# Attention and an MLP mixer on one core: ten of 18 channel-MLP token groups deferred, and run as seven block products

## The chip, the cores and the metric

The kernel runs on one core of a Trainium2 chip. The core has a tensor engine (PE in the profile; its weight loads are listed apart as PEld), VectorE (DVE), ScalarE (ACT), GpSimd (POOL) and SyncE (SP), which here only issues DMAs; ScalarE issues DMAs too. Each engine works through its own queue in order and waits on semaphores. Matmuls write PSUM, which VectorE and ScalarE read. The metric is the time of one execution in microseconds on the device, the median of several runs.

## The reference

All arrays are float32 (the weights reach the device as they are stored on the host). Eight batches, eight heads, 576 tokens, head size 64.

```python
scores = scale * q @ k.T                      # (8, 8, 576, 576)
thresh = max(scores, -1) - tau
scores = where(scores >= thresh, scores, -1e9)
attn   = softmax(scores)                      # sum + 1e-9
x = (attn @ v) with heads side by side        # (8, 576, 512)

h  = relu(x.T @ w_tok1) @ w_tok2              # token MLP, 576 -> 256 -> 576
u  = x + h.T
h2 = relu(u @ w_ch1) @ w_ch2                  # channel MLP, 512 -> 1536 -> 512
out = u + h2
```

## The kernel before

The order of the work is written out by hand and kept as written. Attention is cut into 144 **units** of 128 query rows and two heads: 8 batches x 2 halves x 9. One turn of the main loop (`for u in range(...)`) does, for unit u:

- `scores(u)` (L306): score matmuls into two PSUM tiles; VectorE takes the row maximum (L311), GpSimd makes the bias (L312).
- `norm(u-1)` (L335 to L339): reciprocals on VectorE, products on GpSimd.
- `fill(0.4)`: channel and token MLP steps (below).
- `turn_blocks(u-2)`: VectorE transposes the weights of unit u-2 within 32x32 blocks into a third of the tile T (L369). After every third unit SyncE issues 16 DMAs, each a block row and column of T, into eT (L378); there is one eT buffer.
- `weigh(u)`: two ScalarE passes (L321, L328), with three times `fill(0.2)` between and behind them.
- loads of q and k for later pairs on ScalarE's queue (L105), of v on SyncE's (L114).
- `values(...)`: for a set of three units, two turns after its `turn_blocks`, the value products on the tensor engine (L413, L418), which read eT; ScalarE copies them to xT, the activations x transposed (L423).

In batch 0 the transposes go over the tensor engine (L357), not over DMAs.

After a batch's last value product `push(b)` makes its later work a list of steps, each with a cost in us written in the code: the token MLP (`token_mlp`: five transposes L449, two first-layer steps L456, eight second-layer steps L466 with an add on VectorE, L470; 18.8 in all), mixed with what is left of the list, and then groups of 256 tokens of the **channel MLP** (`channel_mlp`). Two batches lie side by side in xT: 1152 tokens, four groups and a half. An even batch adds the first two groups, an odd batch the other two and a half. A group has twelve steps `ch1` (four matmuls of 256 columns, L509, and a Relu on ScalarE, L510; cost 1.7 each) and eight steps `ch2` (three matmuls of 512 columns, L530, cost 2.6 each; after four of them an add on VectorE, L542, and the store, L549): 41.4. At its second `ch1` the group's activations are turned on VectorE (L493) and moved by 16 DMAs on SyncE (L499).

`fill(share)` adds `share * quota` to a credit and issues steps until the credit is used up. The quota is set by `push`, so that `KEEP` is left when the next batch's steps come:

```python
    KEEP = 45.0
    KEEP_FIRST = 20.0
        ...
        quota = (sum(c for c, _ in todo) - (KEEP if b else KEEP_FIRST)) / (UB - 1)
```

UB is 18, a batch's units. `push(0)` runs in turn 20, `push(b)` for later b at the end of turn 18b + 21 (39 for batch 1). After the loop `fill(1.0)` issues all that is left: the last batch's token MLP, the leftover and the groups (6, 2), (6, 3) and the half group (6, 4), which `ch2_last` (L557, L564, L569) ends.

Of the kernel before, what the change touches and what calls it, by code (L numbers as in the profile page):

```python
# [21 lines left out]
def kernel(  # L22
# [43 lines left out]
    SCALE = 1.0 / 8.0  # L66

    const = ctx.enter_context(tc.tile_pool(name="const", bufs=1))
    ld = ctx.enter_context(tc.tile_pool(name="ld", bufs=2))
    work = ctx.enter_context(tc.tile_pool(name="work", bufs=2))  # L70
    small = ctx.enter_context(tc.tile_pool(name="small", bufs=6))
    ps_sc = ctx.enter_context(tc.tile_pool(name="ps_sc", bufs=2, space=bass.MemoryType.PSUM))
    ps_tr = ctx.enter_context(tc.tile_pool(name="ps_tr", bufs=2, space=bass.MemoryType.PSUM))


# [19 lines left out]
    def load_qk(n, eng, parts=range(8), blocks=(range(S // 32),) * 2):  # L95


        b, p = pairs[n]
        if n not in loaded:
            loaded[n] = [ld.tile([P, S // 32, 32], F32, tag=tag, bufs=1, name=f"{tag}_{n}") for tag in ("lq", "lk")]  # L100
        for part in parts:
            i, which = divmod(part, 2)
            h, c = divmod(i, 2)
            lo, hi = blocks[which].start, blocks[which].stop
            eng[which].dma_start(  # L105
                out=loaded[n][which][32 * i : 32 * i + 32, lo:hi],
                in_=(q, k)[which][b, 2 * p + h, 32 * lo : 32 * hi, 32 * c : 32 * c + 32].rearrange("(n t) d -> t n d", t=32),
            )

    def load_v(n):  # L110

        b, p = pairs[n]
        lv = ld.tile([P, NK, D], F32, tag="lv", bufs=4, name=f"lv_{n}")
        nc.sync.dma_start(out=lv, in_=v[b].rearrange("h s d -> (h s) d")[2 * S * p : 2 * S * p + 2 * S, :].rearrange("(c p) d -> p c d", p=P))  # L114
        vals[n] = lv

# [166 lines left out]

    def prep(n, parts=((0, 0, S // 32), (1, 0, S // 32))):
        if n not in heads:
            heads[n] = [work.tile([P, S], F32, tag=name, name=f"{name}_{n}") for name in ("qT", "kT")]
        for which, lo, hi in parts:
            nc.vector.transpose(
                out=heads[n][which][:, 32 * lo : 32 * hi], in_=loaded[n][which][:, lo:hi].rearrange("p n d -> p (n d)")
            )  # L290
# [24 lines left out]
    def weigh(u):  # L315
        sc, bias = st.pop(u)
        rs = small.tile([P, 2], F32, tag="rs", name=f"rs_{u}")
        e = work.tile([P, 2 * S], F32, tag="e", bufs=3, name=f"e_{u}")
        for h in range(2):
            eh = e[:, S * h : S * h + S].rearrange("p (f x) -> p f x", f=2)  # L320
            nc.scalar.activation(out=eh, in_=sc[h][:, :, 0:HS], func=AF.Prelu, bias=bias[:, h : h + 1], scale=SCALE, alpha=STEEP)  # L321
        st[u] = e, rs

        if b_now:
            fill(0.2)
        for h in range(2):
            eh = e[:, S * h : S * h + S]
            nc.scalar.activation(out=eh, in_=eh, func=AF.Exp, bias=ntau, accum_out=rs[:, h : h + 1])  # L328
            if b_now:
                fill(0.2)  # L330
# [13 lines left out]
    def turn(u, third):  # L344

        b, p0, t = units[u]
        key, place = (b, p0, t // GU), t % GU
        e = st[u]

        if third == 0 and place == 0:  # L350
            eTs[key] = work.tile([P, NK, GU * P], F32, tag="T", name=f"eT_{u}")
        if third == 2:
            st.pop(u)
        ps = ps_tr.tile([P, MAIN], F32, tag="tr", name=f"tr{third}_{u}")[:, 0 : 3 * P].rearrange("p (c x) -> p c x", c=3)
        for c in range(3):
            k0 = (3 * third + c) * P
            nc.tensor.transpose(out=ps[:, c, :], in_=e[:, k0 : k0 + P], identity=ident)  # L357
        on = nc.scalar.copy if third == 1 else nc.vector.tensor_copy
        on(out=eTs[key][:, 3 * third : 3 * third + 3, P * place : P * place + P], in_=ps)

    def turn_blocks(u):
# [2 lines left out]
        key, place = (b, p0, t // GU), t % GU  # L364
        e = st.pop(u)
        if place == 0:
            Ts[key] = work.tile([P, 4, GU, NK * 32], F32, tag="T", name=f"T_{u}")
        T = Ts[key]
        nc.vector.transpose(  # L369
            out=T[:, :, place, :].rearrange("p a (c x) -> p c a x", c=NK), in_=e.rearrange("p (c a x) -> p c a x", c=NK, a=4)  # L370
        )
        if place == GU - 1:
            del Ts[key]
            eT = work.tile([P, GU, 4, NK * 32], F32, tag="eT", bufs=1, name=f"eT_{u}")
            eTs[key] = eT.rearrange("p n i (c x) -> p (n i) c x", c=NK)
            for a in range(4):
                for i in range(4):
                    nc.sync.dma_start(out=eT[32 * a : 32 * a + 32, :, i, :], in_=T[32 * i : 32 * i + 32, a, :, :])  # L378
# [105 lines left out]
    def channel_mlp(b, uT, i):  # L484
# [63 lines left out]
                    nc.vector.tensor_copy(out=o, in_=flat)  # L548
                nc.sync.dma_start(out=out[b : b + 2].rearrange("b s d -> (b s) d")[t0 : t0 + P, :], in_=o)  # L549

        def ch2_last(half):

            t0 = GR * i
            w = DM // 2
            ps = ps_mm.tile([P, w], F32, tag="mm", name=f"c2_{b}_{i}_h{half}")
            for j in range(NJ):
                nc.tensor.matmul(  # L557
                    ps, lhsT=s["g"][:, j, 0:P], rhs=wc2[:, j, w * half : w * half + w], start=(j == 0), stop=(j == NJ - 1)
                )
            if half == 0:  # L560
                move_u()
            o = s["us"][:, half].rearrange("q a x -> q (a x)")[:, 0:w]
            cs = slice(NCC // 2 * half, NCC // 2 * half + NCC // 2)
            nc.vector.tensor_add(  # L564
                out=o.rearrange("q (c k d) -> q c k d", c=NCC // 2, k=4),
                in0=ps.rearrange("q (c k d) -> q c k d", c=NCC // 2, k=4),
                in1=s["ut"][:, 0].rearrange("q k (c d) -> q c k d", c=NCC)[:, cs],
            )
            nc.sync.dma_start(out=out[b : b + 2].rearrange("b s d -> (b s) d")[t0 : t0 + P, w * half : w * half + w], in_=o)  # L569

        if b == B - 2 and n == P:
            return [(0.0067 * n, lambda j=j: ch1(j)) for j in range(NJ)] + [(5.2, lambda half=half: ch2_last(half)) for half in range(2)]
        return [(0.0067 * n, lambda j=j: ch1(j)) for j in range(NJ)] + [
            (2.6 if part or b else 3.0, lambda t=t, part=part: ch2(t, part)) for t in range(nt) for part in range(4)
        ]
# [1 line left out]
    def move_u():  # L577
        while moves:
            moves.popleft()()

    KEEP = 45.0
    KEEP_FIRST = 20.0
# [17 lines left out]
    def push(b):  # L603
# [10 lines left out]
            todo.extend(old[:n] + [step])  # L614
            del old[:n]
        todo.extend(old)
        for i in range(2) if b % 2 == 0 else range(2, (2 * S + GR - 1) // GR):
            todo.extend(channel_mlp(b - b % 2, uT, i))
        quota = (sum(c for c, _ in todo) - (KEEP if b else KEEP_FIRST)) / (UB - 1)


# [26 lines left out]
    for u in range(len(units) + LAG + 4):  # L648
# [88 lines left out]

        if back and wt % GU == 0 or not on:
            move_u()
    need(len(pieces) - 1)  # L740
    quota = 1e9
    fill(1.0)
# [1 line left out]
_INS = ['q', 'k', 'v', 'tau', 'moe_w_tok1', 'moe_w_tok2', 'moe_w_ch1', 'moe_w_ch2']  # L744
_OUTS = [((8, 576, 512), 'float32')]
# [25 lines left out]
```

## Time and profile before

| | us |
|---|---|
| runs: median (lowest to highest of 3) | 1352.09 (1351.51 to 1353.36) |
| profiled execution, first to last instruction | 1349.9 |
| tensor engine busy, first layer of the channel MLP (L509) | 400.1 |
| tensor engine busy, second layer (L530, and L557) | 379.0, 10.5 |
| tensor engine busy, scores (L306) | 190.3 |
| tensor engine busy, value products (L413, L418) | 46.9, 136.8 |
| tensor engine busy, token MLP (L456, L466) | 72.4, 75.2 |
| VectorE row maximum (L311), block transposes (L369) | 204.4, 171.9 |
| ScalarE passes (L321, L328) | 199.8, 221.1 |
| DMA eT<-T: 672 issues, median to landing | 2.3 each |

A line of the profile names the code line, the engine, the operation, and output<-inputs by the program's tile names. Durations of matmuls overlap, since they are pipelined: what one costs is the distance from start to start. A float32 matmul of the code shows as two records. Unit 40 starts at 272.1 us, unit 142 at 1140.3, the last value product ends at 1182.7, and the work up to 1242.7 is the list's leftover and the token MLP of batch 7; then come the last two and a half groups.

### The profile page before, as it was taken

The numbers are of one execution on the slowest core, as the hardware profiler recorded it, in microseconds if no ns is written. First come the engines' busy times: TensorE is split into PE (matmuls) and PEld (weight loads), VectorE is DVE, ScalarE is ACT, GpSimd is POOL, SyncE is SP. The second block draws the span as 40 slices with busy tenths as digits, with TensorE's granted clock in tenths as the row PEclk, the third lists the DMA queues.
The fourth block names the chain that finished last, engine by engine and source line by source line (L and its number), as shares of the span: only waits on it lengthen the run. The fifth ranks groups of instructions, "written<-read, shape, count | busy, mean of one in ns | idle before, by whom it ended". The sixth has DMA issues, their size and how long they took to land.

```text
span 1349.9 us, 17890 instructions
## 1 busy us (share of the span) xinstructions
PE 1306.6 (97%) x6186; PEld 817.1 (61%) x6186; DVE 592.2 (44%) x1026; ACT 585.1 (43%) x1299; POOL 352.5 (26%) x683
## 2 busy tenths in 40 slices
PE   7888899999999999999999999999999999999999
PEld 5565556547474666655665567565656566575677
DVE  6878874445443435434334445434443454201000
ACT  6777654444445435443434444354333454120110
POOL 4565652222222213222222222222221222100000
PEclk8998999999999999999999999999999999999999
DMA  5535764535353544543345435535443453400000
GB/s 123 120 87 127 199 168 97 127 94 136 83 133 89 114 109 96 126 109 88 86 107 125 98 85 123 125 82 115 109 102 83 114 118 79 112 22 17 23 24 32
DMA packets 296746, 135.31 MB, mean 100 GB/s; under 512 B 204816, under 2 KB 289552, under 8 KB 296656
## 3 DMA queue, kind: packets, MB, share of 16 engines
q1 hardware_dynamic: 168944, 118.27, 34.4%
q10 hardware_dynamic: 127712, 15.90, 7.4%
q8 instruction: 49, 0.80, 0.3%
q14 instruction: 41, 0.34, 0.1%
HBM read 43.25 MB, written 9.44 MB: 39 GB/s over the span
## 4 chain that ended last, share of the span: by engine, by line
PE 86%; DVE 6%; DMA 3%; ACT 2%; SPq 1%; issue 1%; POOL 1%; ACTq 0%; DVEq 0%; POOLq 0%
PE c L530 26%; PE c L509 26%; PE sc L306 11%; PE pv L418 9%; PE t L456 5%; PE t L466 4%; PE pv L413 3%; DVE mx L311 2%; PE tx L449 1%; DMA lk<-in_k_dram 1%; ACT e L321 1%; SPq L378 1%; PE c_h L557 1%; DVE T L369 1%; DVE high L211 1%
## 5 line engine op out<-in xcount | busy, mean ns | idle before, releaser
L509 PE MATMUL c<-xT,wc 128*128 128x256 f32 (+1 forms) x1920 | 400.1, 362 | 0.1
L311 DVE TENSOR_REDUCE mx<-sc 128x1 f32<-128x576 f32 x288 | 204.4, 750 | 444.3 <-PE sc L306 443.2
L530 PE MATMUL c<-wc,g 128*128 128x512 f32 x840 | 379.0, 597 | 0.0
L509 PEld LDWEIGHTS c<-xT,wc 128*128 128x128 f32 x1920 | 334.9, 191 | 69.3 <-issue 29.7
L312 POOL TENSOR_SCALAR bias<-mx,toff 128x1 f32<-128x1 f32 x288 | 81.1, 282 | 775.6 <-DVE mx L311 722.7
L321 ACT ACTIVATE e<-sc,bias 128x576 f32<-128x576 f32 x288 | 199.8, 739 | 182.5 <-POOL bias L312 176.7
L530 PEld LDWEIGHTS c<-wc,g 128*128 128x128 f32 x840 | 154.7, 190 | 176.1 <-issue 172.4
L328 ACT ACTIVATE e<-e,ntau 128x576 f32<-128x576 f32 x288 | 221.1, 771 | 0.0
L339 POOL TENSOR_SCALAR e<-e,rr 128x576 f32<-128x576 f32 x288 | 214.3, 756 | 14.8 <-ACT g L510 2.6
L510 ACT ACTIVATE g<-c 128x256 f32<-128x256 f32 (+1 forms) x240 | 86.7, 361 | 296.5 <-PE c L509 283.4
L306 PE MATMUL sc<-kT,qT 64*128 64x288 f32 (+1 forms) x1280 | 190.3, 433 | 6.9 <-ACT e L321 5.9
L369 DVE STREAM_TRANSPOSE T<-e 128x1152 f32<-128x1152 f32 x126 | 171.9, 1364 | 5.5 <-DMA eT<-T 2.9
L306 PEld LDWEIGHTS sc<-kT,qT 64*128 64x128 f32 (+1 forms) x1280 | 105.2, 178 | 92.2 <-issue 57.2
L418 PE MATMUL pv<-eT,lv 128*64 128x384 f32 (+1 forms) x1024 | 136.8, 408 | 0.0
L418 PEld LDWEIGHTS pv<-eT,lv 128*64 128x64 f32 x1024 | 76.9, 138 | 49.9 <-issue 42.1
L423 ACT COPY xT<-pv 128x384 f32<-128x384 f32 (+1 forms) x56 | 21.0, 400 | 164.6 <-PE pv L418 159.5
L466 PE MATMUL t<-w,a 128*128 128x288 f32 x256 | 75.2, 421 | 8.2 <-DVE xT L470 4.8
L542 DVE TENSOR_TENSOR us<-c,ut 128x512 f32<-128x512 f32 x26 | 17.9, 690 | 137.5 <-PE c L530 122.7
L456 PE MATMUL t<-x_sb,w 128*128 128x512 f32 (+1 forms) x180 | 72.4, 549 | 0.0
L466 PEld LDWEIGHTS t<-w,a 128*128 128x128 f32 x256 | 45.9, 192 | 30.2 <-issue 10.5
L470 DVE TENSOR_TENSOR xT<-xT,t 128x288 f32<-128x288 f32 x64 | 28.3, 446 | 70.6 <-PE t L466 69.9
L328 ACT ACTIVATION_READ_ACCUMULATOR e<-e,ntau 128x1 f32 x288 | 56.7, 197 | 0.0
(51 smaller groups left out, 571.2 us busy)
## 6 DMA issues: line engine op xcount, KB each, us to landing
eT<-T SPq DMA_DIRECT2D x672, 108.0 KB, 2.3
scratch<-in_moe_w_ch_dram SPq DMA_DIRECT2D x24, 512.0 KB, 3.7
lv<-in_v_dram SPq DMA_DIRECT2D x32, 288.0 KB, 3.5
out_dram<-us SPq DMA_DIRECT2D x35, 256.0 KB, 2.2
lk<-in_k_dram ACTq DMA_DIRECT2D x109, 72.0 KB, 2.7
lq<-in_q_dram ACTq DMA_DIRECT2D x106, 72.0 KB, 2.3
ut<-us SPq DMA_DIRECT2D x192, 32.0 KB, 1.9
lk<-in_k_dram SPq DMA_DIRECT2D x19, 72.0 KB, 3.2
```

The costliest lines, as they stand in the source:

```text
L306: nc.tensor.matmul(sc[h][rows, f, 0:HS], lhsT=qT[r, cols], rhs=kT[r, HS * f : HS * f + HS], start=True, stop=True)
L311: nc.vector.tensor_reduce(out=mx[:, c], in_=sc[h][:, :, 0:HS], axis=AX.XY, op=ALU.max)
L321: nc.scalar.activation(out=eh, in_=sc[h][:, :, 0:HS], func=AF.Prelu, bias=bias[:, h : h + 1], scale=SCALE, alpha=STEEP)
L328: nc.scalar.activation(out=eh, in_=eh, func=AF.Exp, bias=ntau, accum_out=rs[:, h : h + 1])
L339: nc.gpsimd.tensor_scalar(out=eh, in0=eh, scalar1=rr[:, h : h + 1], scalar2=1.0, op0=ALU.mult, op1=ALU.mult)
L369: nc.vector.transpose(out=T[:, :, place, :].rearrange("p a (c x) -> p c a x", c=NK), in_=e.rearrange("p (c a x) -> p c a x", c=NK, a=4))
L418: nc.tensor.matmul(to[r], lhsT=lv[:, j, :], rhs=e[j], start=False, stop=(c == NI - 1), skip_group_check=True)
L456: nc.tensor.matmul(to, lhsT=w1[:, t, P * m : P * m + P], rhs=x_sb[:, t, cols], start=(t == 0), stop=(t == NT - 1))
L466: nc.tensor.matmul(to, lhsT=a[:, m, P * c : P * c + P], rhs=w2[:, m, HS * f : HS * f + HS], start=(m == 0), stop=(m == NTK - 1))
L509: nc.tensor.matmul(ps, lhsT=wc1[:, j, c, :], rhs=uT[:, c, GR * i : GR * i + n], start=(c == 0), stop=(c == NCC - 1))
L510: nc.scalar.activation(out=s["g"][:, j, 0:n], in_=ps, func=AF.Relu)
L530: nc.tensor.matmul(flat, lhsT=s["g"][:, j, P * t : P * t + P], rhs=wc2[:, j, :], start=(j == 0 and b > 0), stop=(j == NJ - 1), skip_group_ ...
```

## The change

Only eight of the groups are still put into the list (`NOW`). The rest, ten groups' worth of tokens, waits: groups of finished batches are written to device memory (`spill`, at the end of a turn, on SyncE), those of the last batch pair stay in xT. After attention the tiles of attention are given up (`attn.close()`; its pools now lie on the right side of the memories), and the waiting tokens are taken in five blocks of 512. Both layers of a block are products of 2 x 2 blocks, and each is made of seven block products and sums instead of eight products: for `ch1(j)` seven pairs of matmuls of 256 columns, 6 x 14 in a block; for `ch2` seven parts of six matmuls of 256 columns, twice. Sums of weights and of activations are made on VectorE ahead (`sums`, the two in-place `sub` calls, `sums_u`), sums of products while they are in PSUM. Two of the accumulators (`y` and `z`) are read after their first product and then added to by a second one. The last addition of u is made on GpSimd (`late_add`). `ch2_last` goes. KEEP, the quota's formula and the main loop's order stay.

```diff
-    ld = ctx.enter_context(tc.tile_pool(name="ld", bufs=2))
+    attn = ctx.enter_context(ExitStack())
+    att = attn.enter_context(tc.tile_pool(name="att", bufs=2, side="right"))
+    ps_sc = attn.enter_context(tc.tile_pool(name="ps_sc", bufs=2, space=bass.MemoryType.PSUM, side="right"))
+    dram = ctx.enter_context(tc.tile_pool(name="dram", bufs=1, space=bass.MemoryType.DRAM))
...
+    NOW = {(0, 0), (0, 1), (0, 2), (2, 0), (2, 2), (4, 0), (4, 2), (6, 0)}
+    kept = deque()
+    spilled = {}
+
+    def spill():
+
+        while kept:
+            b, i = kept.popleft()
+            n = min(GR, 2 * S - GR * i)
+            d = dram.tile([P, NCC, n], F32, name=f"spill_{b}_{i}")
+            nc.sync.dma_start(out=d, in_=xTs[b][:, :, GR * i : GR * i + n])
+            spilled[b, i] = d
...
-        for i in range(2) if b % 2 == 0 else range(2, (2 * S + GR - 1) // GR):
-            todo.extend(channel_mlp(b - b % 2, uT, i))
+        ready = [(b - b % 2, i) for i in (range(2) if b % 2 == 0 else range(2, (2 * S + GR - 1) // GR))]
+        if b < B - 1:
+            todo.append((0.0, lambda: kept.extend(g for g in ready if g not in NOW)))
+        for g in ready:
+            if g in NOW:
+                todo.extend(channel_mlp(g[0], uT, g[1]))
         quota = (sum(c for c, _ in todo) - (KEEP if b else KEEP_FIRST)) / (UB - 1)
...
+        spill()
     need(len(pieces) - 1)
+    attn.close()
+    end = ctx.enter_context(tc.tile_pool(name="end", bufs=1, side="right", reuse_waits="tile"))
+    ps_x = ctx.enter_context(tc.tile_pool(name="ps_x", bufs=4, space=bass.MemoryType.PSUM, side="right", reuse_waits="tile"))
+    HJ, HC, HD = NJ // 2, NCC // 2, DM // 2
...
+    groups = [
+        [(0, 3), (2, 1)],
+        [(2, 3), (4, 1)],
+        [(4, 3), (6, 1)],
+        [(6, 2), (6, 3)],
+        [(0, 4), (2, 4), (4, 4), (6, 4)],
+    ]
...
+        def sums_u(self):
+            t = self.t = end.tile([P, 4, HC, GR], F32, tag="t", name=f"t_{self.n}")
+            sub(t[:, 0], self.block(0, 1), self.block(0, 0))
+            sub(t[:, 1], self.block(1, 1), t[:, 0])
+            sub(t[:, 2], self.block(1, 1), self.block(0, 1))
+            sub(t[:, 3], self.block(1, 0), t[:, 1])
...
+        def ch1(self, j):
...
+            self.product(y, list(zip(w(0, 0), u(0, 0))))
+            nc.scalar.copy(out=p1, in_=y)
+            self.product(x4, list(zip(w(1, 1), us(3))))
+            self.product(y, list(zip(w(0, 1), u(1, 0))), False)
+            nc.scalar.activation(out=c11, in_=y, func=AF.Relu)
+            self.product(x6, list(zip(ws(1), us(1))))
+            add(u2, x6, p1)
+            self.product(x7, list(zip(w(1, 0), us(2))))
+            add(u3, x7, u2)
+            self.product(z, list(zip(ws(0), us(0))))
+            add(c21, x4, u3)
+            add(c22, z, u3)
+            self.product(z, list(zip(ws(2), u(1, 1))), False)
+            nc.scalar.activation(out=self.gb[:, j, :], in_=self.gb[:, j, :], func=AF.Relu)
+            add(c12, z, u2)
+            nc.scalar.activation(out=c12, in_=c12, func=AF.Relu)
...
+        def ch2(self, m, part):
...
+            elif part == 5:
+                self.z = self.psum("tr", f"oz_{self.n}_{m}")
+                prod(self.z, s[:, 0], w2s[:, 0])
+                add(o(1, 1), four(self.z), four(u3))
+                late_add(1, 1)
+                store(1)
+            else:
+                prod(self.z, s[:, 2], side2(1, 1), start=False)
+                add(o(0, 1), four(self.z), four(u2))
+                late_add(0, 1)
+                store(0)
+
+    lates = [Late(n) for n in range(len(groups))]
+    lates[0].load()
     quota = 1e9
+    rest = list(todo)
+    todo.clear()
+    for step in rest:
+        todo.append(step)
+        if sums:
+            todo.append((0.0, sums.pop(0)))
     fill(1.0)
+    sub(side1(1, 0), side1(0, 0), side1(1, 0))
+    sub(side2(0, 1), side2(1, 1), side2(0, 1))
...
+    lates[0].sums_u()
+    for late in lates:
+        if late.n + 1 < len(lates):
+            lates[late.n + 1].load()
+        for j in range(HJ):
+            late.ch1(j)
+            if j in (1, 3):
+                late.turn_u(j // 2)
+        for m in range(2):
+            for part in range(7):
+                late.ch2(m, part)
+                if m == 0 and part == 4 and late.n + 1 < len(lates):
+                    lates[late.n + 1].sums_u()
```

`side1` and `side2` are views of a quarter of the weights wc1 and wc2; `add` and `sub` are VectorE tensor operations; `product` issues the matmuls of one block product. `turn_u` turns the activations of half a block and moves them with 16 DMAs on SyncE, as before for a group.

## The prediction

> **What bounds the kernel now.** I read the page's busy shares and slices first, then the chain, then the tensor engine's, SyncE's and VectorE's timelines where attention runs with little other work, and last the windows around long waits.
>
> ```profile
> span 1349.9 us, 17890 instructions
> PE 1306.6 (97%) x6186; PEld 817.1 (61%) x6186; DVE 592.2 (44%) x1026; ACT 585.1 (43%) x1299; POOL 352.5 (26%) x683
> PE   7888899999999999999999999999999999999999
> PEclk8998999999999999999999999999999999999999
> ...
> PE 86%; DVE 6%; DMA 3%; ACT 2%; SPq 1%; issue 1%; POOL 1%; ACTq 0%; DVEq 0%; POOLq 0%
> ```
>
> The tensor engine (PE) bounds the whole: from slice 6 on it is busy at 90% or more. So fewer products look like time saved. But that holds because channel products fill every wait of attention, and the change takes most of them out of there. What attention costs without them must be read where filling was thinnest, in batch 1:
>
> ```profile
> 228.61 1.24 PE L306 MATMUL sc<-kT,qT 64*128 64x288 f32 x8
> 229.78 3.72 PE L509 MATMUL c<-xT,wc 128*128 128x256 f32 x16
> ...
> 247.99 0.55 PE L413 MATMUL pv<-eT,vl 128*64 128x192 f32 x4 [1.76 <-DMA lq<-in_q_dram]
> ...
> 251.39 0.51 PE L306 MATMUL sc<-kT,qT 64*128 64x288 f32 x2
> ```
>
> ```profile
> 232.93 12.72 SPq L378 DMA_DIRECT2D eT<-T  x16
> ```
>
> Three units make a cycle. Scores of its first unit start at 228.61; VectorE's third transpose T of the set ends at 232.9, 4.3 us later; then SyncE issues 16 moves eT<-T one after the other; the value product needs all of them and starts at 247.99, with PE idle for 1.76 us. The lq named there is a DMA whose landing the burst shares a wait with; the last move was issued at about 245.1 and lands 2.3 us later (page row of eT<-T), which is the wait. Scores of the next cycle stand behind the value product on PE's queue. So this cycle is a loop of 22.8 us that no arithmetic sets. An undisturbed burst is hardly shorter:
>
> ```profile
> 272.14 1.20 PE L306 MATMUL sc<-kT,qT 64*64 64x288 f32 x16
> ...
> ```
>
> ```profile
> 276.44 10.32 SPq L378 DMA_DIRECT2D eT<-T  x16
> ```
>
> 10.32/16 = 0.645 us each, whatever PE does. Over the trace's 42 bursts, first issue to last landing is 11.9 to 15.5 us, mean 13.2 (moves held behind q and k loads make the difference).
>
> **The loop's length.** 4.3 + 13.2 + 0.3 (landing to product) + 3.4 (value product, 247.99 to 251.39) = **21.2 us per cycle**. PE's own work per cycle is three scores (1.17 each, 228.61 to 229.78), 3.4, and three quotas: 6.9 + 3 x quota. The quota follows from push() with the code's own costs (token MLP 18.8, a full group 41.4, 42.2 in the first batch pair):
> - Batch 1, both kernels: about 4.6, work 20.7. Just below the loop, as the trace shows.
> - Before, later: 5.0 in batch 2, then 5.5 and 7.0 in turn; work 21.9 to 27.9. PE sets the pace, the burst is covered.
> - After, batch 2: (6.2 left + 18.8 + 42.2 - 45)/17 = 1.3; work 10.8.
> - After, batches 3 to 7: (41.5 + 18.8 + 41.4 - 45)/17 = 3.3; work 17.1 (17 x 3.3 of 18 leaves the 41.5 again).
> So the loop takes over as the bound in every cycle after push(1), which runs at the end of unit 39; the cover that hid the bursts is gone.
>
> **The sum, against the profiled 1349.9.**
> 1. Up to the scores of unit 40: **272.1**, unchanged.
> 2. Units 40 to 141, 34 cycles x 21.2 = **720.8**. Before, they end near 1140.
> 3. Clock. Waits of PE rise to 4 us a cycle (21.2 - 17.1), in batch 2 to about 6 (its three units can't go faster than 3.9 each, since scores wait for Prelu to empty their PSUM). The rows of a 4.4 us wait at 107:
>
> ```profile
> 107.00:111.00 4.00, 0.00 (x0) 0.00 (x0) 3.90 (x9) 2.08 (x4) 0.89 (x4) 0.98 0.94 234
> 111.00:118.00 7.00, 6.72 (x25) 3.15 (x27) 5.87 (x9) 5.08 (x12) 4.03 (x4) 0.52 0.43 102
> ```
>
>    The seventh number after the stretch's busy times, 0.98 and 0.52, is the granted clock: a wait of 4.4 us was paid with some 6.8 us at half speed, 3.4 us of work. Waits of 1.8 (at 157.7 and 246.2) cost nothing. Bounds 0 and 3.4 per cycle; waits of 4 lie nearer the costly row, but only the part on value product and scores counts, so 0.5 for 28 cycles and 2.0 for the six of batch 2: **26**. Below nothing is excluded: waiting gives no clock.
> 4. Units 142 to the last value product: one more loop, then a burst that waits for the single eT buffer: 21.2 + 13.2 + 0.3 + 3.4 = **38.1**.
> 5. Leftover group and token MLP of batch 7: **60.0**, as from 1182.7 to 1242.7 now. The six VectorE sums of weights are put among its first steps and are hidden by it.
> 6. Handover. VectorE has behind the last leftover step its add (0.69, row of L542), two in-place differences of 1536 columns and four of 512. From 0.425 at 256 columns (L564) and 0.69 at 512: 1.75 and 0.69, sum 6.95; PE covers it with one product pair of 0.86, and halves its clock after. 6.3 + 1.7 = **8.0**.
> 7. The five blocks. Rates come from the end of the kernel before, first eight and then six records between neighbours:
>
> ```profile
> 1211.80 1.89 PE L509 MATMUL c<-xT,wc 128*128 128x256 f32 x8
> 1213.52 1.13 PE L466 MATMUL t<-w,a 128*128 128x288 f32 x4
> ...
> 1220.73 2.74 PE L530 MATMUL c<-wc,g 128*128 128x512 f32 x6
> 1223.31 1.13 PE L466 MATMUL t<-w,a 128*128 128x288 f32 x4
> ```
>
>    1.72/4 = 0.43 a product of 256 columns, 2.58/3 = 0.86 of 512 (two records each). A block: first layer 6 x 14, second 2 x 42, 168 x 0.43 = 72.2; five, 361.2. The same work before: 10 x (48 x 0.43 + 24 x 0.86) = 412.8 and 2.8 for half groups. The saving of an eighth, 54, is real in products. Against it, z is read by VectorE between its two products with no work between them on PE, 30 times in the first layer and 10 in the second. What such a turn costs:
>
> ```profile
> 301.51 0.78 DVE L470 TENSOR_TENSOR xT<-xT,t 128x288 f32<-128x288 f32 x2
> ...
> 301.98 1.24 PE L466 MATMUL t<-w,a 128*128 128x288 f32 x4 [1.26 <-DVE xT L470]
> ```
>
>    Matmul drain 0.17 (mean 0.597 less spacing 0.43), start 0.04, add 0.425, release 0.05, slower first matmul 0.11: 0.79. Four times VectorE does the next block's sums first (4 x 0.65): 1.7. So 36 x 0.79 + 4 x 1.7 = 35.2. The other waits (y after ScalarE's copy) have a product pair between and about 0.1 to spare; if they miss, 30 x 0.8 more. Sum **396.4**, only 19 below the work it replaces.
> 8. After the last matmul: 3.1 now, and a GpSimd add of 256 columns, about 0.75 (half of L225's 1.43 for 512): **3.9**.
>
> Spills (nine, at most 512 KB, one issue each), their loads and the turns of us (0.6 us an issue, 20 us per block of 79) stand on SyncE outside the bursts, at nothing; a spill just ahead of a burst would cost its transfer, about 3 us, once a batch.
>
> Sum 1525.3, and 2.2 outside the span (1352.1 less 1349.9): **1528 us**.
>
> **Two rules of the Trainium skill.** The page "DMA: Bandwidth & Descriptors", section "Issuing engines are not separate DMA queues", calls the time in which a sequencer initiates a DMA usually small relative to the DMA itself; here 0.645 us stand against 2.3 to landing, and sixteen in a row outlast it four times. By the rule the first rival below would hold; the row decides. "TensorE: Matmul & The Clock Gate", section "HAM oscillation — how this bites in real kernels", speaks against the change: waits beyond about 3.4 us re-throttle in every turn, some 1.7 us each; estimated from it, 34 x 1.7 = 58 in place of 26, so about 1560.
>
> **Rivals.** With L for the loop and no clock loss, the sum is 738 + 36 x L (34 loops, and in step 4 two less 4.3).
> - *The burst is covered after all* (other side, **1342**). If a move were issued in 0.35 us, as the output's store is, the burst takes 15 x 0.35 + 2.3 = 7.6 and L is 15.6; batch 2 takes 6 x 15.6, the rest 28 x 17.1, the end 26.9. It decides from L of 17.1, a burst of 9.1. For it: PE at 97%. Against: none of 42 bursts is below 11.9. Chance 0.06.
> - *Partly covered*, 1353 to 1450: PE's work spread so that shorter loops appear. Against: 19.9, the loop with the shortest burst, gives **1455**. 0.09 below that.
> - *Clock halves in every cycle*, 3.4 each: 1501.5 + 115.6 = **1617**. For it, the 107 row; against, the waits of 1.8 us that went free, and waits that spread below 4. 0.07 for over 1600.
> - *Products of 256 columns are slow* for want of weight loads, so the change doesn't save: L557, 24 products in 10.5 us, says 0.44. It would add 2%, 7 us, inside the range.
>
> **Chances.** Forecast (1450 to 1600) 0.78. From no change a measurement here tells 0.2%: faster 0.06, within 0.01, slower 0.93. Range 1455 to 1600: shortest bursts without clock loss up to most of the throttled case.
>
> **What will show it.** Cycles of about 21 us, value products waiting 3 to 6 us for eT<-T, SyncE's bursts unchanged at 10.3 or more; the last value product ending near 1057 and the five blocks taking some 396 to 400 with 0.8 us before each second z product. I am wrong if attention's cycles come near 17 us, or if the blocks hold waits other than z's.

## The result, and the profile after

The changed kernel takes **1580.16 us** (median of four runs, 1578.04 to 1581.34) against 1352.49 before: ratio 1.168, interval 1.167 to 1.170. It is slower by 228 us. The page of its profiled execution:

```profile
span 1576.3 us, 18436 instructions
PE 1344.8 (85%) x6198; PEld 892.9 (57%) x6198; DVE 732.2 (46%) x1293; ACT 596.1 (38%) x1285; POOL 380.8 (24%) x713
...
PE   7888999675788889788788878788989999999998
...
PEclk8999999777998999899899989999999999999999
...
PE 59%; DMA 13%; DVE 11%; SPq 9%; ACT 4%; issue 3%; POOL 1%; ACTq 0%; POOLq 0%; DVEq 0%
...
L416 PE MATMUL pv<-eT,vl 128*64 128x384 f32 (+1 forms) x256 | 61.1, 556 | 138.5 <-DMA eT<-T 113.7
L421 PE MATMUL pv<-eT,lv 128*64 128x384 f32 (+1 forms) x1024 | 178.4, 500 | 0.0
...
eT<-T SPq DMA_DIRECT2D x672, 108.0 KB, 2.4
```

Three things are to be seen. The tensor engine, 97% busy before, reads 5 to 8 in nearly all of slices 8 to 28, which are attention from unit 40 on: there it waits. The chain of waits, 86% tensor engine before, now goes through DMA and SyncE's queue (SPq) for 22% of the span. And at the value product, which had hardly a wait, the tensor engine stands idle for 138.5 us, 113.7 of them put down to the moves eT<-T, though one move lands about as soon as before (2.4 us against 2.3). The same line of the kernel before, from unit 40 to 1243 us, has 0.9 us:

```profile
L413 PE MATMUL pv<-eT,vl 128*64 128x384 f32 (+1 forms) x192 | 33.3, 425 | 0.9 <-DMA lk<-in_k_dram 0.5 <-DMA out_dram<-us 0.4
```

The granted clock also has 7 in three slices that read 9 before.

Where the time went, by stretches of the two traces (us):

| | before | after |
|---|---|---|
| to the scores of unit 40 | 272.1 | 272.6 |
| units 40 to 141, 34 cycles of three units | 868.2 | 791.1 |
| unit 142 to the last value product | 42.4 | 42.0 |
| leftover and token MLP of batch 7 | 60.0 | 59.7 |
| what follows (before: two and a half groups; after: ten groups' worth) | 107.2 | 410.9 |

The list lost seven and a half groups, of about 41 us each by the code's costs and by the trace alike, some 310 us; the stretch that carried them became only 77 us shorter. Behind attention 304 us were added, close to the same 310. So nearly the whole loss is this: the work was taken out, and its time stayed. One cycle shows how. The tensor engine first, then SyncE's DMA issues in the same stretch; the columns are start, duration, and in brackets the idle time before:

```profile
530.82 0.91 PE L416 MATMUL pv<-eT,vl 128*64 128x192 f32 x4 [5.45 <-DMA eT<-T]
531.52 2.72 PE L421 MATMUL pv<-eT,lv 128*64 128x192 f32 x16
...
535.79 1.24 PE L309 MATMUL sc<-kT,qT 64*128 64x288 f32 x8
...
552.31 0.87 PE L416 MATMUL pv<-eT,vl 128*64 128x384 f32 x4 [1.65 <-DMA eT<-T]
552.98 2.78 PE L421 MATMUL pv<-eT,lv 128*64 128x384 f32 x16
555.69 1.20 PE L309 MATMUL sc<-kT,qT 64*64 64x288 f32 x16
```

```profile
540.11 10.27 SPq L381 DMA_DIRECT2D eT<-T  x16
```

From the first scores of a cycle (535.79) it is 4.3 us to the third T and the burst's first issue (540.11), 12.2 to its last landing and the value product (552.31), and 3.4 to the next scores (555.69). That is the loop, 19.9 us here. The value product of the cycle before shows the second half of the story: after an idle time of 5.45 us it took 4.97 us to the next scores (530.82 to 535.79), not 3.38. The windows of the trace say why; after the busy times of the five engines stands the granted clock. First a window of the kernel before, then three of the change:

```profile
300.00:350.00 50.00, 48.23 (x255) 33.08 (x254) 24.96 (x46) 24.84 (x57) 14.51 (x31) 1.00 0.47 106
```

```profile
300.00:350.00 50.00, 32.41 (x153) 18.29 (x152) 22.64 (x38) 22.63 (x49) 13.81 (x30) 0.76 0.53 111
...
600.00:650.00 50.00, 43.87 (x206) 26.20 (x201) 22.84 (x42) 20.86 (x46) 12.84 (x28) 0.86 0.48 97
...
1200.00:1250.00 50.00, 47.31 (x216) 40.39 (x214) 20.53 (x35) 5.04 (x12) 3.92 (x4) 1.00 0.08 22
```

In batch 2 (300 to 350) the tensor engine is busy for 32 of 50 us, at a clock of 0.76; in the blocks (1200 to 1250) the clock is full again. Between unit 40 and the last value product the trace has 33 stretches at half speed, 174 us in all, and 26 of the 34 value products up to unit 141 run partly in one.

The blocks begin with the handover, and in every first-layer step z is read between its two products:

```profile
1165.66 1.03 PE L830 MATMUL hmm<-u,wc 128*128 128x256 f32 x4
1172.47 2.07 PE L830 MATMUL hx<-t,wc 128*128 128x256 f32 x4 [5.79 <-DVE t L763]
...
1177.63 1.03 PE L830 MATMUL hz<-t,w1s 128*128 128x256 f32 x4
1179.18 1.13 PE L830 MATMUL hz<-u,w1s 128*128 128x256 f32 x4 [0.52 <-DVE spare L760]
```

The handover costs 5.8 us of idle and a stretch at half speed (2.07 for a product that takes 1.03). The two z products start 1.55 us apart, where neighbours start 0.86 apart: 0.68 more, and the product behind them starts another 0.10 late. That is 0.78 per turn in the first layer; in the second layer it is 0.78 six times and 1.92 four times, where VectorE makes the next block's sums first. All 40 turns together take 36 us.

### The profile page after: what moved, and what is told of

It is laid out like the page before. It is cut to its first block, busy times and chain, and to the rows that moved or that the text cites. A ratio compares the mean times of both kernels' runs of the same rounds, so it can differ in the third digit from the quotient of the medians.

```text
span 1576.3 us, 18436 instructions
## 1 busy us (share of the span) xinstructions
PE 1344.8 (85%) x6198; PEld 892.9 (57%) x6198; DVE 732.2 (46%) x1293; ACT 596.1 (38%) x1285; POOL 380.8 (24%) x713
## 4 chain that ended last, share of the span: by engine, by line
PE 59%; DMA 13%; DVE 11%; SPq 9%; ACT 4%; issue 3%; POOL 1%; ACTq 0%; POOLq 0%; DVEq 0%
PE pv L421 10%; PE o L830 8%; SPq L381 8%; PE sc L309 7%; PE c L512 7%; DMA eT<-T 6%; PE hx L830 5%; PE c L533 4%; DMA lk<-in_k_dram 4%; PE t L459 3%; PE pv L416 3%; PE hmm L830 3%; DMA lq<-in_q_dram 3%; PE oz L830 3%; DVE mx L314 3%
## 5 line engine op out<-in xcount | busy, mean ns | idle before, releaser
L324 ACT ACTIVATE e<-sc,bias 128x576 f32<-128x576 f32 x288 | 200.7, 740 | 141.2 <-POOL bias L315 139.3
L512 PE MATMUL c<-xT,wc 128*128 128x256 f32 x768 | 183.2, 387 | 1.0 <-DVE xT L473 0.5
L416 PE MATMUL pv<-eT,vl 128*64 128x384 f32 (+1 forms) x256 | 61.1, 556 | 138.5 <-DMA eT<-T 113.7
L421 PE MATMUL pv<-eT,lv 128*64 128x384 f32 (+1 forms) x1024 | 178.4, 500 | 0.0
L533 PE MATMUL c<-wc,g 128*128 128x512 f32 x384 | 177.7, 605 | 0.5 <-DVE xT L473 0.5
L372 DVE STREAM_TRANSPOSE T<-e 128x1152 f32<-128x1152 f32 x126 | 172.0, 1365 | 6.4 <-DMA eT<-T 4.1
L512 PEld LDWEIGHTS c<-xT,wc 128*128 128x128 f32 x768 | 143.4, 192 | 32.8 <-issue 11.4
L421 PEld LDWEIGHTS pv<-eT,lv 128*64 128x64 f32 x1024 | 103.3, 173 | 71.7 <-issue 58.1
L909 POOL TENSOR_TENSOR us<-us,ut 128x256 f32<-128x256 f32 x30 | 26.3, 878 | 470.9 <-DVE us L760 470.9
L533 PEld LDWEIGHTS c<-wc,g 128*128 128x128 f32 x384 | 70.6, 191 | 82.0 <-issue 78.2
L760 DVE TENSOR_TENSOR spare<-hx,spare 128x256 f32<-128x256 f32 x90 | 38.2, 425 | 94.4 <-PE hx L830 93.4
L830 PE MATMUL hx<-t,wc 128*128 128x256 f32 x240 | 62.6, 384 | 5.8 <-DVE t L763 5.8
```

The source lines that it names most:

```text
L372: nc.vector.transpose(out=T[:, :, place, :].rearrange("p a (c x) -> p c a x", c=NK), in_=e.rearrange("p (c a x) -> p c a x", c=NK, a=4))
L416: nc.tensor.matmul(to[r], lhsT=vl[:, r], rhs=e[NI], start=True, stop=False, skip_group_check=True)
L421: nc.tensor.matmul(to[r], lhsT=lv[:, j, :], rhs=e[j], start=False, stop=(c == NI - 1), skip_group_check=True)
L512: nc.tensor.matmul(ps, lhsT=wc1[:, j, c, :], rhs=uT[:, c, GR * i : GR * i + n], start=(c == 0), stop=(c == NCC - 1))
L533: nc.tensor.matmul(flat, lhsT=s["g"][:, j, P * t : P * t + P], rhs=wc2[:, j, :], start=(j == 0 and b > 0), stop=(j == NJ - 1), skip_group_ ...
L830: nc.tensor.matmul(ps, lhsT=l, rhs=r, start=start and x == 0, stop=x == len(pairs) - 1, skip_group_check=not start)
```

## The experiments

The theory: attention's cycle is a loop (scores, three units, burst of 16 moves, value product, scores) that no arithmetic sets, and the filling that covered it is gone. The rivals: lost clock is the main cost; the seven products themselves are slow; a shorter burst would do as well as cover.

**1 and 2. The value products one turn later, in the changed kernel and in the kernel before.** A value product is no longer due in the turn in which its burst lands, so the next scores don't stand behind it.

```diff
-                due.append((u + (2 if in_blocks(wb) else 1), wb, wp, g))
+                due.append((u + (3 if in_blocks(wb) else 1), wb, wp, g))
```

> The changed kernel with one figure altered: a set's value products stand one turn later in the tensor engine's order (three turns behind the set's last transpose, not two). Same arithmetic, same number of moves, same deferred blocks. Theory A (the loop scores, transpose, burst of 16 moves, value product bounds attention): VectorE's transposes of the next set now run ahead of the value product, so 4.3 us and a unit's scores leave the loop; it falls from 23.3 us measured to burst 13.6 + 0.3 + 3.4 = 17.3, PE's own work is 17.1, waits get short and the clock stays up; attention from unit 40 takes about 34 x 17.5 = 595 in place of 791, and the whole about 1380 us. Rival B (bandwidth: spills and moves crowd the DMA engines): the burst is what it was and grows when sets come closer, little is gained, above 1520. Rival C (too little filler as such, whatever the order): no change, 1580.

> The kernel before with the same figure altered. Theory A: there PE's own work per cycle is above the loop from batch 2 on, so only the few cycles of batch 1 that waited gain: 1345 to 1355 us, within 0.5% of before. Rival C: the same. If it gains more than 1%, the loop bound the kernel before as well and my reading of it as covered was wrong.

In the changed kernel: 1471.15 us, ratio 1.087 (1.084 to 1.090). Cycles fell from 23.3 to 20.0 us and half-speed time from 174 to 72. In the kernel before the same edit cost 0.75% (0.5 to 1.0), somewhat more than the 0.5% allowed for: its last value product ends 10.6 us later, 5.0 of them lost before unit 40, and it gains nothing. So the loop is real, and it bounds the one kernel and not the other. But the 1380 that was expected did not come. SyncE, then the tensor engine, in one cycle of the changed kernel with this edit:

```profile
798.18 11.39 SPq L502 DMA_DIRECT2D ut<-us  x16
809.68 10.24 SPq L381 DMA_DIRECT2D eT<-T  x16
```

```profile
822.72 0.90 PE L416 MATMUL pv<-eT,vl 128*64 128x384 f32 x4 [3.69 <-DMA lk<-in_k_dram]
823.39 4.47 PE L421 MATMUL pv<-eT,lv 128*64 128x384 f32 x16
827.79 1.24 PE L309 MATMUL sc<-kT,qT 64*128 64x288 f32 x8
```

The burst now follows the value product, because there is one eT buffer and the product must have read it: the waits hold 137.4 us of L381 behind L421. Where the 16 moves of u stand on the queue at that moment, the burst comes 11 us later still. The loop changed its shape: burst, one turn of slack, value product, burst. A second eT buffer wasn't tried.

**3. The clock alone.** Seven unread matmuls of 256 columns ahead of each value product of batches 1 to 7 keep the tensor engine busy through the wait.

```diff
+            if in_blocks(b):
+                idle = ps_tr.tile([P, MAIN], F32, tag="tr", name=f"idle_{u}")
+                for x in range(7):
+                    nc.tensor.matmul(idle[:, 0:DTOK], lhsT=ident, rhs=w1[:, 0, :], start=True, stop=True)
             values(b, p0, g)
```

> The changed kernel with seven float32 matmuls of 256 columns that nobody reads (3.0 us at full clock) ahead of each value product of batches 1 to 7, where PE waits. If the halved clock after each wait lengthens the loop (measured 5.0 us from value product to next scores, 3.4 at full clock), these return to 3.4 and the whole falls by about 34 x 1.6 = 54 us, to some 1525 us, less what the added work costs where the wait is shorter. Rival: the clock does not matter to the loop, no change or slower by up to 30 us.

1575.40 us, ratio 1.164 (1.160 to 1.169): almost nothing. Two cycles of it on the tensor engine:

```profile
439.19 3.19 PE L640 MATMUL idle<-w,ident 128*128 128x256 f32 x14
442.43 0.87 PE L416 MATMUL pv<-eT,vl 128*64 128x384 f32 x4
443.10 2.78 PE L421 MATMUL pv<-eT,lv 128*64 128x384 f32 x16
445.81 1.24 PE L309 MATMUL sc<-kT,qT 64*128 64x288 f32 x8
...
460.95 3.19 PE L640 MATMUL idle<-w,ident 128*128 128x256 f32 x14
464.68 0.55 PE L416 MATMUL pv<-eT,vl 128*64 128x192 f32 x4 [0.55 <-DMA eT<-T]
```

The value product is back at 3.4 us (442.43 to 445.81), half-speed time fell from 174 to 65 us, and the mean from value product to next scores from 4.88 to 3.79: **1.1 us a cycle, some 37 us in 34 cycles, belonged to the clock**. Batch 1, which needed no filling, pays for it: unit 40 starts at 286, 13 us later; and the value product now starts 0.8 us after the landing instead of 0.3, behind bursts that are 0.2 longer. The clock is a cost, not the cause: with most of it back, cycles are still 23.0, and all that it cost on the loop, 1.5 us in 34 cycles, is 51 of the 228 us.

**4. z copied.** z's first product goes ahead of x7's, and ScalarE copies it out, so VectorE's add no longer stands between z's two products (first layer; the second alike).

```diff
+            self.product(z, list(zip(ws(0), us(0))))
+            nc.scalar.copy(out=c22, in_=z)
             self.product(x7, list(zip(w(1, 0), us(2))))
             add(u3, x7, u2)
-            self.product(z, list(zip(ws(0), us(0))))
             add(c21, x4, u3)
-            add(c22, z, u3)
+            add(c22, c22, u3)
```

> The changed kernel with z's first product taken ahead of x7's and copied out of PSUM by ScalarE while x7's runs, so that z's second product finds it read. My eighth step: 40 waits in the blocks (measured 0.68 us x 30 and 1.14 x 10, 32 us) go, five blocks take about 375 us in place of 407, whole about 1548 us. Rival: VectorE's or ScalarE's queue is the next limit there (ScalarE's copy of y has 0.1 us to spare), and less than half of it is gained, above 1562.

1548.24 us, ratio 1.144 (1.141 to 1.147), as expected. The same place in the tensor engine's timeline:

```profile
1178.54 1.03 PE L830 MATMUL hz<-t,w1s 128*128 128x256 f32 x4
1179.40 1.03 PE L830 MATMUL hx<-t,wc 128*128 128x256 f32 x4
1180.27 1.03 PE L830 MATMUL hz<-u,w1s 128*128 128x256 f32 x4
```

Starts 0.86 apart, no brackets: the turn is gone. The blocks took 375.7 us instead of 406.3, 31 us less. The turns on z were 36; some 5 come back as a new delay of 0.2 us a step at y's second product, whose weight load now waits for ScalarE's copy of y (L866: 25 times, 8.6 us).

**5. Eight plain products in the blocks**, the same tokens deferred: no sums, no second product into a read accumulator, the second layer 512 columns wide.

```diff
+            for ps, i, n, to in ((y, 0, 0, c11), (x4, 0, 1, c12), (x6, 1, 0, c21), (x7, 1, 1, c22)):
+                self.product(ps, list(zip(w(i, 0) + w(i, 1), u(0, n) + u(1, n))))
+                nc.scalar.activation(out=to, in_=ps, func=AF.Relu)
```

> The changed kernel with the same groups deferred and the same five blocks of 512 tokens, but each block by eight products: no sums, no seven-product scheme, no GpSimd add; second layer 512 columns wide as in the kernel before. It takes the seven products away and leaves the deferral. By my terms the blocks then take 5 x 192 x 0.43 = 413 us in place of 406 and the handover of 7 to 8 us goes: 1575 to 1582 us, no difference from the change that matters, so the deferral alone carries the loss and the seven products gain nothing net. Rival: the seven products are worth their eighth (54 us), then this run comes near 1625; or they cost more than they save, then below 1565.

1580.21 us, ratio 1.170 (1.168 to 1.172): the time of the change itself. The blocks start without a handover and run without a wait, 413.4 us in all:

```profile
1161.05 1.89 PE L830 MATMUL hmm<-u,wc 128*128 128x256 f32 x8
1162.77 5.34 PE L830 MATMUL hx<-u,wc 128*128 128x256 f32 x24
```

So the deferral alone carries the whole loss. The seven products as written, handover included, take 7 us less than eight (406.3 against 413.4) where an eighth would be 52; in the total even that is lost, since attention, whose order is the same in both, ended 4.6 us earlier here; why wasn't looked into. With z copied they are worth 38 us in the blocks.

**6 to 9. A shorter burst.** Eight of the sixteen moves are issued on ScalarE's queue, behind `weigh` (run 6); that with z copied and KEEP at 20, which leaves more filling in attention (run 7); all of it and the later value products (run 8); four of sixteen (run 9).

```diff
+                    if a < 2:
+                        block(nc.sync, a, i)
+                    else:
+                        second.append(lambda a=a, i=i: block(nc.scalar, a, i))
...
+        while second:
+            second.popleft()()
```

> The changed kernel with the 16 moves of each burst shared: eight on SyncE as before, eight on ScalarE's queue, behind its two passes of that turn. Same bytes, same order on the tensor engine. Theory A2 (the loop is long because one queue issues 16 moves at 0.645 us each): SyncE's eight land 7.5 us after the transpose, ScalarE's eight some 8 to 9 us after it, so the loop is about 4.3 + 8.5 + 0.3 + 3.4 = 16.5 us, below PE's own 17.1; cycles from 23.3 to about 18, half-speed stretches mostly gone, the whole about 1580 - 34 x 5.3 = 1400 us. Rival B (the DMA engines' bandwidth, spills included, sets the burst): the burst stays near 13.6 and the whole above 1540. A cost that could eat part: ScalarE issues for some 5 us a cycle and its next Prelu waits, so scores wait too.

> The same without moving the value products: cycles near 17.9, last part longer: 272 + 34 x 17.6 + 38 + 35 + 8 + 375 + 6 = about 1333 us. If the burst is still in the loop by 1 us more, 1367.

> The changed kernel with the shared burst, the value products one turn later, z copied by ScalarE, and KEEP 20 in place of 45 (25 us of the leftover move from behind attention into batch 2, whose quota rises from 1.3 to 2.8). Theory A2: no loop above PE's work, 17.4 a cycle, 16 in batch 2: 272 + 96 + 487 + 35 + 35 + 8 + 375 + 6 = about 1315 us, 3% faster than before. If SyncE or ScalarE is the next limit (as SyncE was with the value products later, where the activations' 16 moves stood ahead of a burst), 1340 to 1380.

> The changed kernel with four of the sixteen moves of a burst on ScalarE's queue in place of eight, twelve on SyncE. Issue time theory: twelve take 7.7 us, burst about 10.3 with holds, and ScalarE is held some 3 us, inside the wait; cycles about 23.3 - 3 = 20.3 us, whole about 1480. If ScalarE's hold is again carried into the scores, 1540 to 1600.

| | us | ratio (interval) | burst, first issue to last landing | cycle |
|---|---|---|---|---|
| the change | 1580.16 | 1.168 (1.167 to 1.170) | 13.7 | 23.3 |
| half on ScalarE | 1633.71 | 1.209 (1.207 to 1.212) | 10.7 | 24.1 |
| half, z copied, KEEP 20 | 1593.33 | 1.180 (1.178 to 1.182) | 11.0 | 24.3 |
| the same, values later | 1650.46 | 1.222 (1.220 to 1.224) | 10.0 | 25.8 |
| a quarter on ScalarE | 1518.93 | 1.124 (1.121 to 1.127) | 11.9 | 21.3 |

(Bursts and cycles are means over units 40 to 141.) The first three missed by 230 to 340 us, and all show one reason. The burst did shrink: in the run with half of the moves, first and last issue lie 6.9 us apart instead of 10.8, though a single move now lands after 3.5 us instead of 2.4. So issuing, more than the transfer, had set its length. But ScalarE issues no faster than SyncE (medians of 0.62 and 0.64 us in that run), and while it does, it computes nothing. ScalarE in the run with half of the moves, then the tensor engine:

```profile
500.84 6.49 ACTq L382 DMA_DIRECT2D eT<-T  x7
...
508.67 1.37 ACT L324 ACTIVATE e<-sc,bias 128x576 f32<-128x576 f32 x2 [7.65 <-DMA eT<-T]
```

```profile
502.21 1.89 PE L520 MATMUL c<-xT,wc 128*128 128x256 f32 x8
509.46 2.91 PE L309 MATMUL sc<-kT,qT 64*128 64x288 f32 x8 [5.37 <-ACT e L324]
```

Seven issues, with their holds, take 6.5 us; the scaling of the scores (L324) waits 7.65 us for its engine, and the next scores 5.37 for the PSUM tiles that it empties. The loop was cut at one place and lengthened at another: over the whole execution the scores wait 170 us for L324 here, 148 and 193 in the next two runs, 32 in the change. And some 31 to 35 us of each run's time are lost before unit 40, which starts at 303.7 to 307.5 us instead of 272.6: batch 1 pays for the issues too. With a quarter (four issues) the burst gives 1.8 us and the scores lose less (62 us of waits): 61 us better than the change, where 100 were expected. The run with half, z copied and KEEP 20 stays 13 us above the change although z copied alone gave 32. A shorter burst helps, then, but no way of issuing it that was tried makes up for the cover.

**10 and 11. Fewer groups deferred.** Only the last two blocks are left: groups (6, 2), (6, 3) and the four half groups. With KEEP as it was and z as in the change (run 10), and with z copied and KEEP rising from 20 by 4 a batch (run 11).

```diff
-    NOW = {(0, 0), (0, 1), (0, 2), (2, 0), (2, 2), (4, 0), (4, 2), (6, 0)}
+    NOW = {(b, i) for b in range(0, B, 2) for i in range(4)} - {(B - 2, 2), (B - 2, 3)}
...
-        [(0, 3), (2, 1)],
-        [(2, 3), (4, 1)],
-        [(4, 3), (6, 1)],
```

> The changed kernel with only the last two blocks deferred, nothing else altered (KEEP 45, z as in the change). Batch 2 has a quota of 3.8, work 18.3 a cycle, below the loop, and loses some 4 us in each of six cycles; from batch 3 on 5.9, work 24.5, covered. 1352 - 5 (168 against two blocks of 81.5) + 8 + 1 + 21 = about 1375 us; without the loss in batch 2, 1355.

> The changed kernel with only the last two blocks deferred (groups (6, 2), (6, 3) and the four half groups; fourteen of eighteen groups run between attention's units as before), z copied by ScalarE, and KEEP rising from 20 by 4 a batch, so that the quota is 5.3 to 5.4 in every batch from 2 on. PE's work per cycle is then 6.9 + 16 = 23, above the loop of 21 to 23, so the bursts are covered again; what is left of the change is two blocks of 73 us for 168 us of the same work, 22 saved, less 8 for the handover and 1 at the end: 1335 to 1346 us, about 1% faster than before. Rival (attention is slow for another cause of the changed kernel, such as its memory layout or the spills): above 1380.

1374.03 (ratio 1.018, 1.015 to 1.021), as expected, and 1365.60 (1.011, 1.010 to 1.013), 20 to 30 us above what was expected. With the filling back, the loss is nearly gone: one more sign that cover, not products, decides. Both runs, and run 12, have the memory layout of the change, so the layout isn't what slows attention; the spills weren't taken out alone, but bursts of the change are only 0.4 us longer than before (13.7 against 13.3 from unit 40 on), so they can have lengthened the bursts by 14 us in 34 cycles at most. The second run's missing gain, in the windows of attention, first before, then this run (span, then the tensor engine's busy time):

```profile
272.00:1140.30 868.30, 860.66 (x4120) 526.65 (x4118) 378.78 (x637) 383.94 (x860) 212.75 (x454) 1.00 0.45 105
```

```profile
272.00:1106.60 834.60, 811.93 (x3800) 486.58 (x3796) 374.68 (x632) 376.67 (x828) 213.96 (x454) 1.00 0.52 109
```

Idle time in attention rose from 7.6 to 22.7 us, at full clock: taking three half groups out (56 us less work up to the blocks) freed only 41. Behind it 159.7 us, to the end of the span, stand for four groups' worth, where the kernel before needs 107.2 for two and a half: 52 more. 41 freed and 52 paid make the 12 us by which its span is longer (1361.9 to 1349.9).

**12. Nothing deferred, one block.** Only groups (6, 2) and (6, 3), which the kernel before also does behind attention, become one block of seven products, z copied, VectorE's sums reordered.

```diff
+    NOW = {(b, i) for b in range(0, B, 2) for i in range(5)} - {(B - 2, 2), (B - 2, 3)}
...
-    sub(side1(1, 0), side1(0, 0), side1(1, 0))
-    sub(side2(0, 1), side2(1, 1), side2(0, 1))
...
     lates[0].sums_u()
+    sub(side1(1, 0), side1(0, 0), side1(1, 0))
```

> Nothing is deferred; only groups (6, 2) and (6, 3), which the kernel before also does behind attention, are one block of seven products. z copied by ScalarE; the sums of activations before the in-place differences, the second difference behind ch1(2), so that less stands between the last leftover step and the first products. Theory (the deferral costs through the burst loop, the block itself saves a little): attention as before, unit 142 near 1140, last value product near 1183; half group (6, 4) about 20.6 (107.2 less 4.1 for the tail, five halves); one block at the 73.6 a block of the run with z copied ((375.7 - 7.7)/5), handover about 2.6 (3.5 of sums and add less a product pair of 0.86), tail 4.3: 1242.7 + 20.6 + 2.6 + 73.6 + 4.3 = 1343.8 in the span, so 1346 against 1352, ratio 0.995. Rival (what frames the block, the handover and the tail, costs as much as an eighth of two groups, 10 us, saves): 1352 to 1358. Other rival (the 20 us that the two-block run missed lie in attention and have nothing to do with how much is deferred): 1360 or more, unit 142 past 1150.

1353.01 us, ratio 1.0014 (1.0004 to 1.0025): no gain, and inside the first rival's range. The handover on its tensor engine:

```profile
1270.01 1.03 PE L826 MATMUL hmm<-xT,wc 128*128 128x256 f32 x4
1273.48 2.03 PE L826 MATMUL hx<-t,wc 128*128 128x256 f32 x4 [2.44 <-DVE t L763]
1275.31 1.85 PE L826 MATMUL hmm<-xT,wc 128*128 128x256 f32 x4
1277.00 1.03 PE L826 MATMUL hx<-t,w1s 128*128 128x256 f32 x4
```

The wait was 2.44, close to the 2.6 worked out, but even that was followed by half speed (2.03 and 1.85 for products of 1.03), 1.8 us that the expectation did not have. From the last leftover step to the end this run takes 103.5 us, before 107.2: the block is worth 3.7. Yet attention ended 6.1 us later than in the profile of before, 2.8 of them up to unit 40 (which starts between 272 and 275 in runs that differ only after it) and most of the rest in two places of 1.3 to 1.4 us. The tensor engine's idle time between units 40 and 142 is 2.4 us longer than before, as much as its waits at the value product grew (from 0.9 to 3.3); what delayed those wasn't settled. No kernel of the study beats the one before.

## Why the prediction was right, and which term was mis-sized

The steps of the sum, and what the trace shows (us):

| step | predicted | measured |
|---|---|---|
| 1 to unit 40 | 272.1 | 272.6 |
| 2 and 3, 34 cycles and clock | 720.8 + 26 | 791.1 |
| 4 unit 142 to last value product | 38.1 | 42.0 |
| 5 leftover, token MLP | 60.0 | 59.7 |
| 6 and 7, handover and five blocks | 8.0 + 396.4 | 406.6 |
| 8 after the last matmul | 3.9 | 4.3 |

The mechanism was right: the burst's loop takes over when the filling leaves, and the burst's issuing did not change (10.27 for sixteen). Experiments 1 and 2, 5, and 10 show it from three sides. The measured time lies inside the range, nearer its upper end. Of the 51 us between 1525.3 and 1576.3, 44 lie in steps 2 and 3.

**The clock, step 3, is the mis-sized term.** From the value product to the next scores the mean is 4.88, not 3.4: 1.5 us in 34 cycles are 51, where the prediction took 26. For the six cycles of batch 2 its 2.0 was right (5.38 less 3.38). For the 28 cycles of batches 3 to 7 it took 0.5, a guess between its two rows, and the trace has 1.4. The waits are not the reason: 4 us were expected there, and the mean is 3.2, from 0 to 5.9. But each of the 26 waits of 2.7 us or more, batch 2's included, has a half-speed stretch that covers much of the value product, which is on the loop; the eight of 2.4 or less have none. Experiment 3 took 1.1 of the 1.5 back. The loop term itself was short by 0.5 in the burst (13.7 for 13.2) and 0.1 before it, 17 to 20 us.

Step 4 is 3.9 late for other reasons. Its two bursts took 12.0 us each, less than the 13.2 assumed. But the second one starts 8.0 us after the first value product, not 3.4: VectorE's last transpose (L372) stands behind an add of the token MLP (L473), which waits 8.8 us for a product that stands behind that value product. And the last value product took 5.1 us, at half speed.

Steps 5 to 8 stood within 3 us, and not because errors cancel: z's turns were 35.2 in the prediction and measure 35.8, the handover 8.0 and 7.7, the products alone 361.2 and 362.5. The only waits inside the blocks are z's, as the prediction asked. Three slips of its sums move little: 6.9 + 3 x 3.3 is 16.8, not 17.1, which puts the first rival at 1334; 6.95 less 0.86 is 6.1, not 6.3; and 4 x 0.65 is 2.6, from which the 1.7 of the four longer turns, measured as 1.9, does not follow.

**The rivals.** "The burst is covered after all" falls with cycles of 23.3 us, 30 of 34 with a wait at the value product, and with it "Partly covered". "Clock halves in every cycle" had the mechanism of step 3 and was too high: 26 value products of 34 were hit, and the mean loss on the path is 1.5 us, not 3.4. "Products of 256 columns are slow" falls with experiment 4 (0.86 between pairs).

The Trainium skill, page "TensorE: Matmul & The Clock Gate", section "HAM oscillation — how this bites in real kernels", has a throttled time of about 1.67 us in every turn of a loop with waits of 3 to 5 us, half of it lost. The direction agrees; here the stretches are longer, 174/33 = 5.3 us, and the loss on the loop was 1.5. The prediction's line on it counted the whole 1.7 as loss: its 58 comes near the measured 51 by luck, since with half lost the same estimate gives 28.

The same skill, page "DMA: Bandwidth & Descriptors", section "Issuing engines are not separate DMA queues", says that starting DMAs on several engines saves only the sequencers' issue time. Run 6 agrees that issue time is saved (the burst goes from 13.7 to 10.7), but that time was most of the burst (10.8 of 13.7 from first to last issue), and the second engine's own work paid for it.

## What to carry to other kernels

A tensor engine at 97% does not say that removing its work saves time: ask what loop of waits the work covers, measure that loop (here scores, burst of sixteen issues, value product: 21 to 23 us), and remove filling only down to its length. A move that is issued in 0.65 us and lands in 2.4 costs its issue when sixteen of them follow one another, and it costs as much on another engine, with that engine's work behind it. Count what surrounds a saving in products: of the 52 us that an eighth was worth here, 7 were left as written and 38 once z was read with a product pair between, and a single block kept 3.7 of 10.

## What the runs showed of the hardware

- Waits of 5.45 and 5.79 us were followed by products at half speed, and so, in experiment 12, was one of 2.44 us (2.03 and 1.85 us for products of 1.03), after waits of 1.8 in the kernel before had cost nothing. Between 2.3 and 3.5 us it can go either way: in experiment 4 a wait of 2.34 before a value product was followed by half speed and one of 3.04 was not. The prediction's two rows, 4.4 and 1.8, had left this open.
- ScalarE issues a move no faster than SyncE: medians of 0.62 and 0.64 us in run 6. Seven in a row took it 6.49 us, 0.93 each with their holds, and its next activation waited 7.65 us.
- Two queues that issue side by side shortened the burst by 3 us, not by half of the 10.3 of issuing: first and last issue are still 6.9 us apart, and from the last issue to the last landing it is 3.8 us (10.7 less 6.9), where it was 2.9 (13.7 less 10.8). A single move lands after 3.5 us, 2.4 before the split.
